# GpSimd's share of the softmax exponentials set to zero, with the planner's constants of that variant

## The chip, the cores and the metric

The kernel runs on one core of a Trainium2 chip. Five engines work side by side on it, each through its own list of instructions in order: TensorE (PE; its weight loads are shown as PEld), VectorE (DVE), ScalarE (ACT), GpSimd (POOL) and SyncE (SP), which here only issues transfers. Semaphores tie the lists together. The metric is the device time of one execution in microseconds (us); the profile is of one execution.

## What is computed

Window attention with cross-shaped stripes on an image of 224 x 224 positions with 96 channels. Half of the channels attend within horizontal stripes of 8 rows, the other half within vertical stripes of 8 columns; then one output projection.

```python
qkv = jnp.einsum('bhwc,cd->bhwd', x, wqkv)          # x: 1 x 224 x 224 x 96
q, k, v = (qkv[..., :C].copy(), qkv[..., C:2 * C].copy(), qkv[..., 2 * C:].copy())
scale = C2 ** (-0.5)                                 # C2 = 48
qh = q[..., :C2].reshape(B * nh, sw * W, C2)         # 28 stripes of 1792 positions
...
ah = _softmax(jnp.einsum('bqc,bkc->bqk', qh, kh) * scale, axis=-1)
oh = jnp.einsum('bqk,bkc->bqc', ah, vh).reshape(B, H, W, C2)
...
av = _softmax(jnp.einsum('bqc,bkc->bqk', qv, kv) * scale, axis=-1)
ov = jnp.einsum('bqk,bkc->bqc', av, vv)              # the same on 28 vertical stripes
...
o = jnp.pad(oh, ((0, 0), (0, 0), (0, 0), (0, C2))) + jnp.pad(ov, ((0, 0), (0, 0), (0, 0), (C2, 0)))
return jnp.einsum('bhwc,cd->bhwd', o, wo)
```

So there are 56 stripes, each with scores of 1792 x 1792, and an exponential of every score.

## The kernel before

**Tiles.** Stripes are worked on in 28 pairs (NP), 14 horizontal, then 14 vertical. Both stripes of a pair share an instruction: one lies in partitions 0 to 63, the other in 64 to 127. The queries of a pair are cut into 4 chunks (512, 512, 512, 256 columns), the keys into 14 tiles of 128. A *score tile* is 128 keys by 512 queries for both stripes (or 2 x 128 keys by 256 queries): 128 partitions by 1024 numbers. A pair has 49 of them (NG), the whole kernel 1372.

**A score tile's way.** TensorE loads key weights (`load_weights`, L190) and multiplies (`loaded_matmul`, L194; for the narrow chunk also L724) into two PSUM banks. Then an exponential is taken in one of three ways:
- ScalarE: one Exp instruction (L892) from banks 0 and 1 or 2 and 3 in turn into one of 8 buffers PTA.
- VectorE: five steps (`d_step`, L903 to L910) that build the bits of a bf16 exponential by a polynomial, from banks 4 and 5 into one of 3 buffers PTD. Steps two to four run in SBUF alone.
- GpSimd: VectorE first copies the tile (L1056) out of banks 4 and 5 to the single buffer `zp_sb` in SBUF, and GpSimd does the polynomial in six steps (`p_step`, L976 to L985), whole or in halves, into one of 3 buffers PTP. At most one such tile is under way.

TensorE then multiplies the result with V (`plan_PV`, L853), summing a chunk's 14 key tiles in bank 6 or 7 (the "value sums"); a column of ones in V gives the softmax's denominator. VectorE empties the bank (L937) into `OT_sb`.

**Fills.** Everything else TensorE does is a `Fill`: the projections of the next pair (K and Q, L462; V, L424) and the output projections of this one (L573, L612). A fill takes the one of banks 6 and 7 that no value sum holds, and its result is taken out by VectorE (L431 for V, L494 and L498 for Q, L506 to L522 for K, L580 and L584 or L618 and L624 for outputs). GpSimd adds the two halves of the output (L647) in the vertical pairs, and SP stores them.

**What sets the order.** The order of each engine is fixed when the kernel is built. A planner walks through an assumed time, and whenever an engine is free in it, asks `pick_act`, `pick_dve`, `pick_pool` or `pick_pe` for its next instruction:
- `pick_pe` takes first ScalarE's next score tile, when its bank is free. Failing that, a tile for GpSimd (while fewer than NPT were given away, L776) or for VectorE (L789), LOOK or LOOKP tiles ahead of ScalarE's; then a value sum, when GRP of them are ready (L816); then a fill. `fits` (L769) lets such work start only if it ends by the time of ScalarE's next tile plus SLACK, or plus DSLACK for VectorE's and GpSimd's tiles.
- Fills have a target before which they don't run and a due time by which they're late (`refill`, L1133): ORD, PACE, DUE1, DUEO, DUES and DUEV set these, and LATE (L815) from when a late one goes ahead of value sums.
- `keep_warm` (L1158) puts spare matmuls into TensorE's gaps when it was idle for more than WARM of the last 3000 ns: a multiplication with zeros added to the open value sum (L1180) or a throw-away product in a free bank (L1199).
- GpSimd's instructions are placed beside VectorE's steps that read PSUM (`safe`, L987), by the assumed time; VectorE's three SBUF steps are held back while the plan has GpSimd busy (L1061).

```python
            if D["cur"] is None and len(P_out) < NZP and D["np"] < NPT and fits(240.0, "r64", DSLACK):
                lo = max(progress(), lastA[0]) + LOOKP
...
            if D["cur"] is None and fits(240.0, "r64", DSLACK):
                G = max(progress(), lastA[0]) + LOOK
...
            late = want_fill and progress() > f.due - LATE and used < NBA - 1
            if ready and fits(235.0) and not late and (len(ready) >= min(GRP, nleft) or used >= NBA - UTH or not want_fill and inburst[0] > 0):
```

When it runs, nothing of the assumed time is left but the order and the semaphores: an instruction waits for what it needs, and those behind it on its engine wait with it.

## Time and profile before

| | |
|---|---|
| three runs | 1096.08, 1096.21, 1099.76 us; median 1096.21 |
| the profiled execution | 1096.08 us, its span 1094.3 us |
| score tiles on ScalarE / VectorE / GpSimd | 1169 / 158 / 45 |
| busy time of GpSimd in its tiles' steps (L976 to L985) | 478.7 us |
| busy time of GpSimd in the output additions (L647) | 105.6 us, 89 instructions |
| VectorE's five steps, mean of one | 1221, 716, 432, 696, 1219 ns |
| TensorE's zeros (L1180) | 34.0 us, 262 matmuls |
| mean granted TensorE clock | 0.993 |

The span runs from the first instruction to the end of the last; the time of the run lies 1.8 us above it. [...] A group's "idle before" is the time its engine stood idle just ahead of the group's instructions, with what ended it.

### The profile page before, as it was taken

The numbers are of one execution on the slowest core, as the hardware profiler recorded it, in microseconds if no ns is written. First come the engines' busy times: TensorE is split into PE (matmuls) and PEld (weight loads), VectorE is DVE, ScalarE is ACT, GpSimd is POOL, SyncE is SP. The second block draws the span as 40 slices with busy tenths as digits, with TensorE's granted clock in tenths as the row PEclk, the third lists the DMA queues.
The fourth block names the chain that finished last, engine by engine and source line by source line (L and its number), as shares of the span: only waits on it lengthen the run. The fifth ranks groups of instructions, "written<-read, shape, count | busy, mean of one in ns | idle before, by whom it ended". The sixth has DMA issues, their size and how long they took to land.

```text
span 1094.3 us, 28704 instructions
## 1 busy us (share of the span) xinstructions
PE 1040.7 (95%) x12104; PEld 372.7 (34%) x12104; DVE 1047.4 (96%) x1712; ACT 1077.2 (98%) x1172; POOL 584.6 (53%) x451
## 2 busy tenths in 40 slices
PE   9999999999999999999999999999999999999997
PEld 2333333332333333233333333333333333333332
DVE  5999999999999999999999999999999999999996
ACT  6999999999999999999999999999999999999997
POOL 0544555453545645364564465656565565656563
PEclk7999999999999999999999999999999999999999
DMA  5301001101110120110111122122222222221111
GB/s 99 69 9 35 19 18 36 36 10 27 36 27 10 35 36 7 30 35 17 20 35 27 35 44 41 39 41 42 41 41 40 39 42 41 39 41 38 24 28 37
DMA packets 169001, 37.37 MB, mean 34 GB/s; under 512 B 168872, under 2 KB 168872, under 8 KB 168872
## 3 DMA queue, kind: packets, MB, share of 16 engines
q1 hardware_dynamic: 167256, 35.35, 17.3%
q8 instruction: 94, 1.54, 0.6%
q10 hardware_dynamic: 1616, 0.18, 0.1%
q14 instruction: 35, 0.29, 0.1%
HBM read 0.15 MB, written 9.63 MB: 9 GB/s over the span
## 4 chain that ended last, share of the span: by engine, by line
ACT 71%; DVE 21%; PE 4%; POOL 1%; issue 1%; DMA 0%; SPq 0%; DVEq 0%; POOLq 0%
ACT PTA L892 71%; DVE tt_sb L903 4%; DVE PTD L910 3%; DVE sq_sb L905 2%; DVE tt_sb L909 2%; PE ps L194 2%; PE ps L853 1%; DVE sq_sb L907 1%; DVE KT_sb L522 1%; DVE zp_sb L1056 1%; DVE tmp L624 1%; DVE OT_sb L937 1%; DVE V_sb L431 1%; POOL PTP L985 1%; DVE QT_sb L498 1%
## 5 line engine op out<-in xcount | busy, mean ns | idle before, releaser
L892 ACT ACTIVATE PTA<-ps 128x1024 bf16<-128x1024 f32 x1169 | 1075.0, 1214 | 5.9 <-PE ps L194 5.1
L194 PE MATMUL ps<-QT_sb,KT_sb 49*64 49x512 bf16 (+3 forms) x5488 | 486.5, 369 | 38.9 <-ACT PTA L892 25.5
L853 PE MATMUL ps<-PTA,V_sb 128*64 128x512 bf16 (+1 forms) x2674 | 422.9, 367 | 0.6 <-DVE Ph_sb L584 0.2
L190 PEld LDWEIGHTS <-KT_sb 49*64 49x64 bf16 (+1 forms) x5488 | 137.4, 103 | 335.0 <-issue 321.9
L903 DVE TENSOR_SCALAR tt_sb<-ps 128x1024 f16<-128x1024 uint16 x158 | 192.9, 1221 | 11.6 <-PE ps L194 7.1
L910 DVE SCALAR_TENSOR_TENSOR PTD<-ps,tt_sb 128x1024 uint16<-128x1024 f32 x158 | 192.5, 1219 | 1.3
L853 PEld LDWEIGHTS ps<-PTA,V_sb 128*64 128x64 bf16 x2674 | 119.8, 108 | 204.1 <-issue 162.8
L647 POOL TENSOR_TENSOR out_sb<-tmp,Ph_sb 128x480 bf16<-128x480 f32 (+2 forms) x89 | 105.6, 1195 | 110.9 <-DVE sq_sb L907 57.9
L978 POOL TENSOR_TENSOR uq_sb<-up_sb 128x1024 f16<-128x1024 f16 (+1 forms) x52 | 101.3, 1952 | 111.6 <-DVE sq_sb L907 57.5
L982 POOL TENSOR_TENSOR up_sb<-uq_sb,up_sb 128x512 f16<-128x512 f16 (+1 forms) x65 | 112.3, 1732 | 84.8 <-DVE sq_sb L907 27.4
L984 POOL TENSOR_TENSOR zp_sb<-zp_sb,up_sb 128x512 f32<-128x512 f32 (+1 forms) x74 | 111.2, 1508 | 54.6 <-DVE sq_sb L907 31.7
L976 POOL TENSOR_SCALAR up_sb<-zp_sb 128x1024 f16<-128x1024 uint16 x45 | 47.1, 1047 | 130.3 <-DVE zp_sb L1056 115.4
L905 DVE TENSOR_TENSOR sq_sb<-tt_sb 128x1024 f16<-128x1024 f16 x158 | 113.1, 716 | 0.1
L909 DVE TENSOR_TENSOR tt_sb<-sq_sb,tt_sb 128x1024 f16<-128x1024 f16 x158 | 109.9, 696 | 2.9
L462 PE MATMUL ps<-xT_sb,w_sb 128*64 128x448 bf16 (+3 forms) x448 | 85.7, 380 | 6.1 <-DVE KT_sb L522 3.0
L937 DVE CAST OT_sb<-ps 128x512 bf16<-128x512 f32 (+5 forms) x118 | 69.3, 591 | 1.4 <-PE ps L853 1.4
L907 DVE TENSOR_SCALAR sq_sb<-sq_sb 128x1024 f16<-128x1024 f16 x158 | 68.2, 432 | 2.2
L1056 DVE COPY zp_sb<-ps 128x1024 f32<-128x1024 f32 x45 | 55.0, 1222 | 8.8 <-POOL PTP L985 4.6
L853 PE MATMUL ps<-PTD,V_sb 128*64 128x512 bf16 (+1 forms) x360 | 62.1, 362 | 0.0
L985 POOL TENSOR_SCALAR PTP<-zp_sb 128x512 uint16<-128x512 f32 (+1 forms) x66 | 57.4, 870 | 5.7 <-POOL zp_sb L984 0.2
L624 DVE TENSOR_TENSOR tmp<-ps,rc 128x480 f32<-128x480 f32 (+2 forms) x92 | 53.2, 578 | 1.1
L522 DVE TENSOR_TENSOR KT_sb<-ps,shift 128x448 bf16<-128x448 f32 (+2 forms) x84 | 51.6, 615 | 2.1 <-PE ps L462 2.1
(55 smaller groups left out, 668.3 us busy)
## 6 DMA issues: line engine op xcount, KB each, us to landing
out_dram<-out_sb SPq DMA_DIRECT2D x389, 24.0 KB, 1.9
xT_sb<-in_x_dram SPq DMA_TRANSPOSE x332, 2.6
w_sb<-in_wqkv_dram ACTq DMA_DIRECT2D x2, 54.0 KB, 3.1
out_dram<-out_sb ACTq DMA_DIRECT2D x3, 24.0 KB, 1.9
wo_sb<-in_wo_dram SPq DMA_DIRECT2D x4, 9.0 KB
wo_sb<-one_sb SPq DMA_DIRECT2D x4, 0.0 KB
```

Source lines behind the costliest of these rows:

```text
L190: return e.add_instruction(mybir.InstLdweights(tile_size=(64, 64), tile_position=pos, name=nc.get_next_instruction_name(), engine=mybir.En ...
L194: return e.add_instruction(mybir.InstMatmult(start_tensor_calc=True, stop_tensor_calc=True, tile_size=(64, 64), tile_position=pos, ldweigh ...
L647: return e.tensor_tensor(out_sb[b][:, wdw, k0:k0 + n, :], tmpi[:, 0:n, :], Ph_sb[:, k0:k0 + n, j, :], ALU.add)
L853: ins = e.matmul(bk[64 * wdw:64 * wdw + 64, 0:qs], lhsT=V_sb[b][:, wdw, kt, :], rhs=pt[:, wdw * 512 + i * qs:wdw * 512 + (i + 1) * qs], st ...
L892: e = add("act", [ev, bufA_ev[sl]], lambda e, base=base, sl=sl: e.activation(PTA[sl][:], ps[:, base * 512:(base + 2) * 512], ACTF.Exp, sca ...
L903: return lambda e: e.tensor_scalar(tt_sb[:], dps.bitcast(U16)[:, 0:2048:2], CS / 65536.0, CS * CA3, ALU.mult, ALU.add)
L905: return lambda e: e.tensor_tensor(sq_sb[:], tt_sb[:], tt_sb[:], ALU.mult)
L909: return lambda e: e.tensor_tensor(tt_sb[:], sq_sb[:], tt_sb[:], ALU.mult)
L910: return lambda e: e.scalar_tensor_tensor(PTD[sl][:].bitcast(U16), dps, CC, tt_sb[:], ALU.add, ALU.add)
L978: return e.tensor_tensor(q, u, u, ALU.mult)
L982: return e.tensor_tensor(u, q, u, ALU.mult)
L984: return e.tensor_tensor(z, z, u, ALU.add)
```

## The change

Only constants at the head of the kernel differ; no function does. NPT = 0 means that no score tile goes to GpSimd. The rest are the planner's: SLACK, WARM and the like keep their value and become floats; DSLACK goes from 120 to 300, GRP from 2 to 3, LOOK from 8 to 10, PACE from 1 to 1.5, LATE from 10 to 5; ORD = 0 puts the first two Q fills ahead of the V fills and reckons due times back from the end of the pair, where ORD = 1 has all K and Q fills due from the pair's beginning. LOOKP is without effect once NPT is 0, and DUE1 and DUEV once ORD is 0; DUEO then counts.

```diff
-    SLACK = 120
-    PACE = 1
+    SLACK = 120.0
+    PACE = 1.5
     FDUE = 20.0
-    DSLACK = 120.0
-    GRP = 2
+    DSLACK = 300.0
+    GRP = 3
     NBA = 8
-    LOOK = 8
-    NPT = 400
+    LOOK = 10
+    NPT = 0
...
-    DUE1 = 0
+    DUE1 = 20.0
     DUEV = 10
-    LATE = 10
+    LATE = 5.0
...
-    ORD = 1
-    LOOKP = 32
-    WARM = 600
+    ORD = 0
+    LOOKP = 16
+    WARM = 600.0
```

The kernel that results from it, as built, has 1195 score tiles on ScalarE, 177 on VectorE and none on GpSimd.

## The prediction

> **What bounds the kernel now.** I read the page first: busy shares, then the chain of waits, then the groups by line, then a window without start and end.

> ```profile
> span 1094.3 us, 28704 instructions
> PE 1040.7 (95%) x12104; PEld 372.7 (34%) x12104; DVE 1047.4 (96%) x1712; ACT 1077.2 (98%) x1172; POOL 584.6 (53%) x451
> ...
> ACT 71%; DVE 21%; PE 4%; POOL 1%; issue 1%; DMA 0%; SPq 0%; DVEq 0%; POOLq 0%
> ...
> L892 ACT ACTIVATE PTA<-ps 128x1024 bf16<-128x1024 f32 x1169 | 1075.0, 1214 | 5.9 <-PE ps L194 5.1
> ...
> L903 DVE TENSOR_SCALAR tt_sb<-ps 128x1024 f16<-128x1024 uint16 x158 | 192.9, 1221 | 11.6 <-PE ps L194 7.1
> ...
> L1056 DVE COPY zp_sb<-ps 128x1024 f32<-128x1024 f32 x45 | 55.0, 1222 | 8.8 <-POOL PTP L985 4.6
> ```

> ```profile
> 30.00:1060.00 1030.00, 986.28 (x11621) 354.66 (x11619) 1004.21 (x1616) 1029.35 (x1122) 565.57 (x422) 1.00 0.17 32
> ```

> The second fence is the window from 30 to 1060 us: PE, PEld, DVE, ACT, POOL busy, then the granted clock, 1.00. ScalarE is never idle there (1029.35 of 1030), VectorE hardly (97.5%). ScalarE's busy time hides small losses, because its instructions overlap: one lasts 1214 ns on average, yet the next starts earlier. The timeline shows by how much.

> ```profile
> 8.40 1.94 ACT L892 ACTIVATE PTA<-ps 128x1024 bf16<-128x1024 f32 x2 [1.03 <-PE ps L194]
> ...
> 1070.79 1.83 POOL L985 TENSOR_SCALAR PTP<-zp_sb 128x512 uint16<-128x512 f32 x2
> ...
> 1071.58 0.57 DVE L907 TENSOR_SCALAR sq_sb<-sq_sb 128x1024 f16<-128x1024 f16 x1
> ...
> 1072.18 0.97 DVE L909 TENSOR_TENSOR tt_sb<-sq_sb,tt_sb 128x1024 f16<-128x1024 f16 x1
> ...
> 1072.68 0.41 PE L853 MATMUL ps<-PTP,V_sb 128*64 128x512 bf16 x2 [0.60 <-POOL PTP L985]
> ...
> 1073.46 14.77 ACT L892 ACTIVATE PTA<-ps 128x1024 bf16<-128x1024 f32 x16 [0.18 <-PE ps L194]
> ...
> 1078.24 0.68 DVE L909 TENSOR_TENSOR tt_sb<-sq_sb,tt_sb 128x1024 f16<-128x1024 f16 x1
> ```

> Sixteen score tiles in 14.77 us, less 1.21 for the last, are 13.56 / 15 = 0.904 us from start to start; no interval of the 1168 in the trace is shorter, and over half equal it. That is ScalarE's floor. The first tile starts at 8.40, the last at 1073.46 + 14.77 - 1.19 = 1087.04, so 1168 intervals took 1078.6 us where the floor is 1055.9: 22.8 us are lost. The 14th tile starts at 25.50 (the long ScalarE stretch of the chain begins there), so 17.10 - 13 x 0.904 = 5.4 us of it are lost at the start and 17.4 later. The fence also shows two ways of losing: TensorE waits 0.60 us for a tile from GpSimd, and the score tile queued behind it comes late; and a GpSimd instruction over SBUF-only VectorE work stretches L909 from 0.68 to 0.97.

> **What is removed.** NPT = 0 takes away all of GpSimd's 45 score tiles: on VectorE 45 copies (L1056), on GpSimd 353 half- or full-tile steps (L976 to L985, 479 us busy), on TensorE 51 pairs of value-sum matmuls that read PTP. The built program shows who inherits them. ScalarE's tiles go from 1169 to 1195, VectorE's own from 158 to 177: 26 + 19 = 45. TensorE's matmuls are the same but for zeros (131 to 180 pairs at L1180) and padding (8 to 15 at L1199). All projection and output work, SP's queue and its order are identical.

> **ScalarE's sum.** 26 more tiles at the floor: 26 x 0.904 = +23.5 us. Nothing can cover it, since the engine has no idle time in the window above. [...]

> **VectorE's sum.** A copy holds it 1.14 us (start to next start, back to back): 45 x 1.14 = -51.3. A tile of its own holds it 1.140 + 0.609 + 0.343 + 0.609 + 1.132 = 3.83 (medians of L903, L905, L907, L909, L910, the same way): 19 x 3.83 = +72.8. GpSimd's overlaps go: L905 lasts 685 ns alone and 853 under L985 (21 times), 866 under L980 (6); L907 422 alone, 504 under L985 (12); L513 328 alone, about 960 under GpSimd (5). With the few L909 like the one above that is some 11 us; the 89 additions L647 stay and keep 2, so -9. Its waits for GpSimd's single zp_sb buffer and around the copies (7.7 in all) go, and the rest of its mid-span waits (18.2) grow with 177/158, +2.2. Sum: -51.3 + 72.8 - 9 - 5.5 = +7. So ScalarE asks for 23.5 more and VectorE for 7; ScalarE becomes the clearer bound, and VectorE gets some 16 us of slack.

> [...]

> **The lost 17.4.** A score tile's matmuls (L194) start 50 ns after ScalarE has left their bank, and ScalarE starts 425 ns after they do; with 1231 ns for its own instruction that is 1706 against 2 x 0.904 = 1808: a cover of 0.10 us. TensorE runs in order, so whatever is late in front of a score tile by more eats ScalarE's time. In the trace 7.8 us of the loss stands behind a TensorE wait that a VectorE instruction ended (KT_sb L522 alone 3.5). The stretches holding a GpSimd tile's value sums lose 1.97 us in 45, where others lose 14 ns each, so 1.3 goes with them for certain. The relief lies between -1.3 and -17.4; I take 1.3 and six tenths of the 7.8, together -6, as VectorE gets slack but keeps its order and its waits.

> **The other constants.** DSLACK (120 to 300), GRP, LOOK, PACE, LATE and ORD move work between the score tiles; I read what stands between two of ScalarE's in TensorE's order. It is still at most two items ("value sum, value sum" 406 times before, 428 after), so no stretch holds more than before. A VectorE score tile stands directly in front of ScalarE's 85 times, against 63. Such stretches lose 5 ns each now. A tile's matmuls hold TensorE 0.21 us (two value-sum pairs take 0.62, one takes 0.41), so with the cover gone each costs 0.11: from 22 x 0.005 = 0.1 to 85 x 0.11 = +9.4. I take +1, by the nearest row, that of the same stretches. Filling work in last place goes from 137 to 146 stretches, 46 ns each against 16 in first place: +0.3, left out. More zeros fill gaps; stretches ending in zeros lose 0 to 9 ns now, so nothing. The bound on all of this below is nought, since a gain is counted in the relief. TensorE's order is the same for the first 14 score tiles, so the 5.4 of the start stays; the end, six microseconds after the last score tile, keeps its work.

> **Sum.** 1094.3 + 23.5 - 6 + 1 = 1112.8 us of span. Around the span lie 1096.08 - 1094.3 = 1.8, and that run is within 0.2 of the median 1096.21. Forecast: **1114.6**.

> **The rivals.**
> - *VectorE's relief goes all to ScalarE.* For it: the chain passes through VectorE for 21%, and VectorE is 97.5% busy. Against it: of 13.3 us in the intervals that lose over 20 ns each, 4.9 stand behind no wait of TensorE for VectorE or GpSimd. The loss falls by 12 to 17.4: 1094.3 + 23.5 - 12 (or 17.4) + 1.8 = 1107.6 to 1102.2.
> - *VectorE's tiles push ScalarE's.* DSLACK 300 lets L789's pick stand closer in front of a score tile; behind it are queued the score tile and the value sums, and for those ScalarE's buffers wait. For it: the 85 places and a cover of only 0.10. Against it: 5 ns each today. With no relief beyond 1.3: 1094.3 + 23.5 - 1.3 + 9.4 + 1.8 = 1127.7; from 1122.
> - *Not slower.* ScalarE's waits all came from the mixed work of three engines, and with GpSimd out it runs at its floor throughout: 1094.3 + 23.5 - 22.8 + 1.8 = 1096.8. Against 0.5% (5.5 us, about what a measurement here can tell from no change) it counts as no change while the whole loss stays under 4.9 us. The start alone loses 5.4 and its order is unchanged.
> - *It does not do what its few words say.* Bank choice (L304), the first four score tiles (L1097) and the zeros (L1172) are in both kernels; only constants differ. That moves no number, as the counts above are of the built programs.

> **How the numbers follow.** Forecast 0.56 (own range 1109 to 1121, from relief of 12 with +1 to relief of 1.3 with 22 x 0.11 = 2.4 pushed: 1119.6 - 11 and + 1.1), relief 0.20, pushed tiles 0.21, not slower 0.03. The range goes from 1104 (leaving the lower third of the relief case and the last one, about 0.1) to 1126 (leaving under half of the pushed case, about 0.1). Slower by over 0.5% means above 1101.7: 0.96; within 0.5%: 0.03; faster: 0.01, since it would need ScalarE under its floor.

> **What would show it.** After: L892 x1195 with the floor interval still 0.904; no L1056 and no L976 to L985; L903 x177; VectorE's share in the middle at 96 to 97%, L905's mean near 690 instead of 716; ScalarE's loss after the 14th tile at 10 to 14 us. It is wrong if the floor moves, if ScalarE loses under 6 or over 24 us there, or if ScalarE waits for anything but score tiles.

## The result, and the profile after

The changed kernel takes 1114.17 us (median of 4 runs, 1113.07 to 1117.7) against 1096.26 for the kernel before (4 runs): ratio 1.0161, with a 95% interval from 1.0130 to 1.0193. The profiled execution took 1115.08 us, its span 1112.8. The forecast was 1114.6 with a span of 1112.8. The span came out as forecast; outside it lie 2.2 to 2.4 us in the four runs of the changed kernel, where the forecast kept the 1.8 of before. What fills that time the traces don't show.

The page of the changed kernel, in the order in which the page of before was read (span, busy times, chain by engine and by line, groups):

```profile
span 1112.8 us, 28395 instructions
PE 1051.7 (95%) x12209; PEld 378.6 (34%) x12209; DVE 1064.1 (96%) x1762; ACT 1098.4 (99%) x1198; POOL 105.4 (9%) x98
...
ACT 97%; PE 1%; DMA 0%; SPq 0%; DVE 0%; issue 0%
...
L892 ACT ACTIVATE PTA<-ps 128x1024 bf16<-128x1024 f32 x1195 | 1096.3, 1299 | 2.7 <-PE ps L194 2.6
...
L903 DVE TENSOR_SCALAR tt_sb<-ps 128x1024 f16<-128x1024 uint16 x177 | 216.2, 1221 | 18.2 <-PE ps L194 12.4
...
L905 DVE TENSOR_TENSOR sq_sb<-tt_sb 128x1024 f16<-128x1024 f16 x177 | 121.3, 686 | 0.5
```

GpSimd has only its output additions left. The chain of waits, of which VectorE had 21% before, is now ScalarE's from end to end (97%). L905 is down from 716 ns to 686; before, it lasted 685 where no GpSimd instruction lay over it.

**The account that should have been made.** The prediction counted ScalarE from start to start. For its row of tiles that is not the right measure, and the prediction's own example shows why: the row of 16 score tiles in 14.77 us. Read one by one in the trace, their starts are 0.904 us apart, but their durations grow from 1018 ns for the second to 1192 for the last, by 12.5 at every tile. A tile that is ready starts a little earlier relative to its predecessor's end each time, and finishes no sooner. From end to end the row gives (14.77 - 1.02) / 15 = 0.917. The timeline of ScalarE near the end of the changed kernel shows the same over 150 tiles:

```profile
968.73 137.93 ACT L892 ACTIVATE PTA<-ps 128x1024 bf16<-128x1024 f32 x150
```

The first of these lasts 1.35 us, so (137.93 - 1.35) / 149 = 0.9166. In both traces the intervals between ends that stay under 925 ns average 0.9166 us (1131 of 1168 before and 1187 of 1194 after are such); eight before and two after are below 914 ns. The starts are 0.904 apart only until a tile lasts some 1357 ns. Then it waits for its bank (50 ns) and its matmuls (425), and 1357 + 50 + 425 = 1832 for two tiles is again 0.916. So the floor is 0.9166, and the same figure stands in the kernel: the planner reckons 917.0 ns for a score tile on ScalarE (L893). The account by ends is (us):

| | before | after |
|---|---|---|
| end of the first score tile | 9.4 | 9.7 |
| further tiles x 0.9166 | 1168: 1070.6 | 1194: 1094.4 |
| lost in the first 13 intervals | 5.2 | 2.5 |
| lost after 30 us | 3.0 | 0.0 |
| after the last score tile | 6.0 | 6.2 |
| span | 1094.3 | 1112.8 |

The change is +0.3 + 23.8 - 2.7 - 3.0 + 0.1 = +18.5. Two terms need a cause: the 3.0 us that went (25 intervals over 940 ns before, none after), and the 2.7 at the start, where TensorE's order is the same in both.

**The start.** A granted clock of 1.00 is called whole here, one of 0.50 half. These are the windows from 0 to 11, 11 to 25 and 25 to 35 us of the kernel before, then 11 to 20 us of the changed one (PE, PEld, DVE, ACT, POOL busy, then the granted clock):

```profile
0.00:11.00 11.00, 8.38 (x58) 3.30 (x58) 3.99 (x18) 4.47 (x6) 1.61 (x9) 1.00 0.68 118
11.00:25.00 14.00, 14.00 (x86) 3.21 (x84) 9.28 (x18) 10.36 (x11) 0.00 (x0) 0.51 0.45 85
25.00:35.00 10.00, 10.00 (x104) 3.11 (x102) 9.00 (x14) 9.94 (x12) 5.37 (x5) 1.00 0.27 51
```

```profile
11.00:20.00 9.00, 8.98 (x66) 2.16 (x66) 5.73 (x12) 7.32 (x8) 0.00 (x0) 0.62 0.44 79
```

The granted clock is at half for 13.65 us in the one (11.09 to 24.74) and for 6.83 in the other (12.04 to 18.87). ScalarE's loss there, 5.2 and 2.5, stands in the same proportion, 0.38 and 0.36 us for each us at half clock. The traces of the experiments below agree. Three more have a half clock at the start: 3.8 us are lost for 10.24 (e3_load_after), 5.1 for 13.65 (e4_load_before) and 2.4 for 6.83 (e8_load30_before). Four have a whole clock there with nothing done to the start (e1_npt0, e2_gp_back, e5_nzp2, e7_load30_after), and lose 0 to 0.2.

### The profile page after: what moved, and what is told of

Its sections match the earlier page's. It is cut to its first block, busy times and chain, and to the rows that moved or that the text cites. A ratio compares the mean times of both kernels' runs of the same rounds, so it can differ in the third digit from the quotient of the medians.

```text
span 1112.8 us, 28395 instructions
## 1 busy us (share of the span) xinstructions
PE 1051.7 (95%) x12209; PEld 378.6 (34%) x12209; DVE 1064.1 (96%) x1762; ACT 1098.4 (99%) x1198; POOL 105.4 (9%) x98
## 4 chain that ended last, share of the span: by engine, by line
ACT 97%; PE 1%; DMA 0%; SPq 0%; DVE 0%; issue 0%
ACT PTA L892 97%; PE ps L194 0%; DMA xT_sb<-in_x_dram 0%; PE ps L853 0%; SPq L201 0%; PE ps L462 0%; PE ps L424 0%; DVE tmp L624 0%; DVE out_sb L647 0%; PE ps L612 0%; PE ps L1199 0%; DVE OT_sb L937 0%; DVE rc L618 0%; PE ps L724 0%
## 5 line engine op out<-in xcount | busy, mean ns | idle before, releaser
L892 ACT ACTIVATE PTA<-ps 128x1024 bf16<-128x1024 f32 x1195 | 1096.3, 1299 | 2.7 <-PE ps L194 2.6
L194 PE MATMUL ps<-QT_sb,KT_sb 49*64 49x512 bf16 (+3 forms) x5488 | 482.7, 364 | 53.4 <-ACT PTA L892 39.2
L853 PE MATMUL ps<-PTA,V_sb 128*64 128x512 bf16 (+1 forms) x2732 | 418.2, 365 | 0.7 <-DVE Ph_sb L584 0.4
L903 DVE TENSOR_SCALAR tt_sb<-ps 128x1024 f16<-128x1024 uint16 x177 | 216.2, 1221 | 18.2 <-PE ps L194 12.4
L910 DVE SCALAR_TENSOR_TENSOR PTD<-ps,tt_sb 128x1024 uint16<-128x1024 f32 x177 | 215.8, 1219 | 2.0
L647 POOL TENSOR_TENSOR out_sb<-tmp,Ph_sb 128x480 bf16<-128x480 f32 (+2 forms) x89 | 103.8, 1181 | 1001.7 <-DVE OT_sb L937 654.9
L853 PEld LDWEIGHTS ps<-PTA,V_sb 128*64 128x64 bf16 x2732 | 118.5, 108 | 194.7 <-issue 142.0
L909 DVE TENSOR_TENSOR tt_sb<-sq_sb,tt_sb 128x1024 f16<-128x1024 f16 x177 | 121.8, 688 | 3.7
L905 DVE TENSOR_TENSOR sq_sb<-tt_sb 128x1024 f16<-128x1024 f16 x177 | 121.3, 686 | 0.5
L907 DVE TENSOR_SCALAR sq_sb<-sq_sb 128x1024 f16<-128x1024 f16 x177 | 74.6, 421 | 2.6
L853 PE MATMUL ps<-PTD,V_sb 128*64 128x512 bf16 (+1 forms) x404 | 70.4, 366 | 0.0
L522 DVE TENSOR_TENSOR KT_sb<-ps,shift 128x448 bf16<-128x448 f32 (+2 forms) x84 | 51.7, 616 | 2.0 <-PE ps L462 1.9
L724 PE MATMUL ps<-QT_sb,KT_sb 49*64 49x256 bf16 (+1 forms) x784 | 53.5, 268 | 0.0
L584 DVE TENSOR_TENSOR Ph_sb<-ps,rc 128x480 bf16<-128x480 f32 x84 | 51.9, 618 | 0.6
L431 DVE CAST V_sb<-ps 128x480 bf16<-128x480 f32 (+1 forms) x84 | 51.7, 617 | 0.3
L1180 PE MATMUL ps<-warm,ident 128*64 128x256 bf16 x360 | 47.5, 283 | 0.0
L462 PEld LDWEIGHTS ps<-xT_sb,w_sb 128*64 128x64 bf16 (+1 forms) x448 | 24.8, 106 | 53.9 <-issue 28.9
L498 DVE SCALAR_TENSOR_TENSOR QT_sb<-ps,biasq 128x448 bf16<-128x448 f32 (+2 forms) x59 | 36.3, 616 | 1.8 <-PE ps L462 1.8
```

Of the source, the lines that this page charges most:

```text
L194: return e.add_instruction(mybir.InstMatmult(start_tensor_calc=True, stop_tensor_calc=True, tile_size=(64, 64), tile_position=pos, ldweigh ...
L462: ins = e.matmul(o, lhsT=wS[0:kr, wblk(P, kind), :], rhs=x_cols(wdw), start=True, stop=True)
L647: return e.tensor_tensor(out_sb[b][:, wdw, k0:k0 + n, :], tmpi[:, 0:n, :], Ph_sb[:, k0:k0 + n, j, :], ALU.add)
L853: ins = e.matmul(bk[64 * wdw:64 * wdw + 64, 0:qs], lhsT=V_sb[b][:, wdw, kt, :], rhs=pt[:, wdw * 512 + i * qs:wdw * 512 + (i + 1) * qs], st ...
L892: e = add("act", [ev, bufA_ev[sl]], lambda e, base=base, sl=sl: e.activation(PTA[sl][:], ps[:, base * 512:(base + 2) * 512], ACTF.Exp, sca ...
L903: return lambda e: e.tensor_scalar(tt_sb[:], dps.bitcast(U16)[:, 0:2048:2], CS / 65536.0, CS * CA3, ALU.mult, ALU.add)
```

## The experiments

In all of them "loss" is ScalarE's time by ends above 0.9166 for each interval. Line numbers shift by one or two where lines were added.

**GpSimd's tiles or the other constants?**

```diff
 # e1_npt0, on the kernel before
-    NPT = 400
+    NPT = 0
 # e2_gp_back, on the changed kernel
-    NPT = 0
+    NPT = 400
-    LOOKP = 16
+    LOOKP = 32
```

> The kernel before with one constant changed, NPT = 0; it has 1195 score tiles on ScalarE, as the changed kernel. Theory A (ScalarE's score tiles end 0.917 us apart whatever stands between them, so the number of its tiles sets the time): 26 x 0.917 = +23.8 us over the kernel before, less up to 3.0 us of its later waits if those came with GpSimd's tiles: 1117 to 1120 us, within 3 us of the changed kernel's 1114.2. Theory B (the other constants, DSLACK and the order of the fills above all, are what made the later waits vanish): ScalarE still loses about 3 us after the first 30 us, at the same kind of places in every fourth pair, and the run is 3 us or more above the changed kernel.

Measured: 1116.35 us (1113.03 to 1118.89), ratio to the kernel before 1.0193 (1.0162 to 1.0225). ScalarE's loss after 30 us is 0.04 us, with every other constant as before. So with the old constants the waits of 3.0 us come and go with GpSimd's tiles, and the other constants aren't needed to remove them.

> The changed kernel with NPT = 400 and LOOKP = 32, so with GpSimd's tiles back and all other constants as changed; it has 1179 score tiles on ScalarE, 165 on VectorE, 28 on GpSimd. Theory A: 16 tiles fewer than the changed kernel, 1114.2 - 16 x 0.917 = 1099.5 us, plus later waits of 0 to 3. Theory B (the other constants cost or gain something by themselves): more than 3 us off that. If waits of ScalarE after 30 us come back, they belong to GpSimd's tiles; if they stay at nought, to the kernel before's own constants.

Measured: 1108.3 us, ratio 1.0141 (1.0100 to 1.0181): 8.8 above theory A's 1099.5, so the count alone did not hold. The timeline of ScalarE shows where it is, and then a window (PE, PEld, DVE, ACT, POOL busy, granted clock):

```profile
153.46 1.02 ACT L892 ACTIVATE PTA<-ps 128x1024 bf16<-128x1024 f32 x1 [0.38 <-PE ps L194]
154.97 1.02 ACT L892 ACTIVATE PTA<-ps 128x1024 bf16<-128x1024 f32 x1 [0.49 <-PE ps L194]
156.53 1.02 ACT L892 ACTIVATE PTA<-ps 128x1024 bf16<-128x1024 f32 x1 [0.54 <-PE ps L194]
```

```profile
152.00:170.00 18.00, 17.56 (x146) 5.64 (x150) 12.76 (x19) 12.19 (x13) 1.84 (x2) 0.53 0.01 2
```

From 152.7 to 169.8 us the clock is at half, score tiles come 1.5 us apart, and ScalarE loses 7.4 us there; elsewhere after the start it loses nothing. The span also ends 2.6 us later behind the last score tile (8.7 us for 6.2). GpSimd's tiles by themselves, 28 of them here, left no waits at a whole clock. So the 3.0 us of the kernel before take both: GpSimd's tiles, and either its own constants or the larger number, 45. These two runs don't tell which of the latter. In the 3 us before 152.7 TensorE waited 0.22 us for KT_sb, 0.31 for ScalarE to leave a bank and 0.77 for OT_sb; what made these late, and whether the clock fell because of them, is open too.

**How much room does VectorE have?** An idle fill of a scratch tile is put into VectorE's list, with no wait and no semaphore, so the order of everything else is untouched.

```diff
                     k = d["k"]
+                    if k == 4 and D["n"] % 3 == 0:
+                        ops["dve"].append(([], lambda e: e.memset(junk[:], 0.0), False))
                     ev = add("dve", ws, d_step(k, sl), D_OCC[k], D_OCC[k] + 107.0)
```

> The changed kernel with 59 idle fills of a scratch tile (128 x 388) put into VectorE's list, one ahead of L910 of every third of its own tiles: 59 x 0.33 = about 19 us more work on VectorE and nothing else. Theory of the forecast (VectorE is 97% busy and near to being the bound, with some 16 us of room): up to 5 us longer. Theory A (only ScalarE sets the pace and VectorE's lateness is caught by the buffers ahead): below 2 us, ScalarE's loss after 30 us still under 2. Rival (VectorE is the bound as well): the whole 19.

> The same idle fills in the kernel before: 53 x 0.33 = about 17 us more work on VectorE. Theory of the forecast (VectorE and ScalarE bound it together, VectorE having hardly any room): 8 to 17 us longer. Theory A (ScalarE sets the pace in the kernel before too, to within 3.0 us of waits after the start): under 4 us longer. The difference between this and the same load in the changed kernel is the room that the change gave VectorE.

The load was smaller than planned: a fill lasted 0.22 us, and no run shows the 0.33 that was expected. So there were 13.0 us of durations in the changed kernel and 11.7 in the kernel before. A fill overlaps its neighbours, so VectorE's busy time rose less, by 4.9 us (1064.1 to 1069.0) and 4.8 (1047.4 to 1052.2). Measured: 1117.7 us (1112.37 to 1122.34) and 1094.42 (ratio to the kernel before 1.0001, 0.9982 to 1.0020). ScalarE's loss after 30 us stays at 0.01 in the first; its profile, of the run of 1116.7, lost 3.8 at the start, at half clock, and the one run with a mean clock of 0.998 took 1112.37. In the second the loss after 30 us goes from 3.0 to 4.2. VectorE, 97.9 and 97.8% busy between 30 and 1060 us, does not set the time by itself in either. The 8 to 17 us for the kernel before were expected of a larger load than this one turned out to be. A larger load (1064 columns for 388) was needed to find the room:

> The changed kernel with larger idle fills on VectorE (128 x 1064), again one ahead of L910 of every third of its tiles: 59 x 0.45 to 0.5 = about 28 us of work, as much as VectorE's idle time between 30 us and the end (27). The smaller load of 8 us left ScalarE's loss there at nought. Theory A: VectorE's room is its idle time, so 0 to 8 us longer. Rival (VectorE co-bound): 15 to 28 us.

> The same larger fills in the kernel before: 53 x 0.45 to 0.5 = about 25 us of work, VectorE's idle time there being 26 us. The smaller load took ScalarE's loss after 30 us from 3.0 to 4.2 us. If GpSimd's tiles made VectorE tight (forecast), this costs clearly more than in the changed kernel: 8 to 20 us. If VectorE had as much room as there: under 8 us.

Measured: 1122.08 us (ratio to the kernel before 1.0276, 1.0242 to 1.0311) and 1106.49 (1.0121, 1.0095 to 1.0146). The page's busy times, the group of the fill, and ScalarE's wait (line, waited for: us, times, longest), of the changed kernel with this load, and then the same of the kernel before with it:

```profile
PE 1050.1 (94%) x12209; PEld 376.9 (34%) x12209; DVE 1081.5 (97%) x1821; ACT 1103.0 (99%) x1198; POOL 105.5 (9%) x98
...
L1077 DVE MEMSET junk<- 128x532 uint32 x59 | 29.6, 502 | 3.5
```

```profile
ACT PTA L893 <- PE ps L195: 2.3, 6, 1.0
```

```profile
PE 1042.9 (94%) x12104; PEld 371.1 (34%) x12104; DVE 1064.0 (96%) x1765; ACT 1083.2 (98%) x1172; POOL 584.0 (53%) x451
...
L1077 DVE MEMSET junk<- 128x532 uint32 x53 | 26.6, 502 | 3.2
```

```profile
ACT PTA L893 <- PE ps L195: 6.8, 21, 1.0
```

ScalarE's loss after 30 us goes from 0.0 to 8.0 us, and from 3.0 to 15.1. VectorE's busy time rose by 17.4 us (1064.1 to 1081.5) and 16.6 (1047.4 to 1064.0). So 9.4 us are hidden in the changed kernel and 4.5 in the kernel before; by the fills' durations, 29.6 and 26.6, it would be 21.6 and 14.5. Either way the change gave VectorE room, an estimated 5 to 7 us from these two loads of unequal size. The kernel before, with 12.1 us more loss, lies where it was expected if GpSimd's tiles made VectorE tight (8 to 20).

**Is the start the clock's doing?** Four throw-away matmuls are put where TensorE stands idle after the first two score tiles; they carry no semaphore, so nothing else moves.

```diff
+        for _ in range(4):
+            ops["pe"].append(([e_warm], lambda e: e.matmul(bank(4)[:, :], lhsT=warm[:, 0:128], rhs=warm[:, :], start=True, stop=True), False))
         for f in [pf0["K"][1], pf0["V"][0]]:
```

> The kernel before with four more throw-away matmuls on zeros in the gap that TensorE has after the first two score tiles; nothing else differs. Theory C (what ScalarE loses in its first 13 intervals, 5.2 us in the kernel before's profile and 2.5 in the changed one's, is the TensorE clock at half for 13.7 and 6.8 us there, which the thin work of the first 11 us brings about or not from launch to launch): the granted clock stays whole at the start in most runs, ScalarE's loss there falls under 1 us, and the median falls by 2 to 5 us with less spread. Rival (the loss is that of the order there, waiting for x and the first projections): unchanged to 1 us.

Measured: ten runs between 1091.5 and 1092.77 us, where 13 of the kernel before beside them lay between 1091.39 and 1095.82, in two heaps: seven up to 1091.83, six from 1093.56. Ratio 0.9989 (0.9977 to 1.0001). The profile has a whole clock and ScalarE loses 0.6 us at the start:

```profile
11.00:25.00 14.00, 13.19 (x138) 4.02 (x138) 12.79 (x24) 13.96 (x16) 2.08 (x2) 1.00 0.46 87
```

Theory C's cause holds: the spread went, and of the runs beside it the seven low ones had a mean granted clock of 0.998 or 0.999, the six high ones 0.993 to 0.997. The median did not fall by 2 to 5 us, as seven of the 13 runs beside it were low ones. With this start the two sides of the change can be compared with a whole clock on both:

> The kernel before with NPT = 0 and the four matmuls at the start: the price of GpSimd's tiles alone, with the clock whole at the start. 26 x 0.917 = +23.8 less the 2.9 us of waits that go: +20.9 over the kernel before with the same start (1091.95): 1112.9, spread under 2 us.

> The changed kernel with the four matmuls at the start. If the other constants do nothing to the time, the same as the run with NPT = 0 alone and this start, 1112.9, to 1 us; ScalarE's loss at the start under 1 us and after 30 us under 0.5.

Measured: 1113.24 us (1112.88 to 1113.81) for the kernel before with NPT = 0, 1113.1 (1112.77 to 1114.1) for the changed kernel, ratios to the kernel before 1.0180 (1.0160 to 1.0201) and 1.0180 (1.0159 to 1.0201). Against 1091.95 that is +21.3 and +21.2 where +20.9 was expected. The 1091.95 comes from another round, on another chip; beside these two runs the kernel before had three with a clock of 0.999, at 1090.95, 1091.46 and 1091.65, and against the middle one it is +21.8 and +21.6. ScalarE loses 1.2 and 0.5 us at the start and 0.04 and 0.01 after 30 us; why 1.2, at a whole clock, is open. With no tile on GpSimd, the other constants together do nothing that these runs can tell.

**More tiles for GpSimd?** If ScalarE's count set the time, giving GpSimd more tiles, or sooner ones that leave ScalarE fewer, should beat both kernels.

```diff
 # e5_nzp2
-    NZP = 1
+    NZP = 2
 # e9_lookp24_start (and 18 in e10_lookp18_start), with the four matmuls at the start
-    LOOKP = 32
+    LOOKP = 24
```

> The kernel before with two zp_sb buffers instead of one (NZP = 2), so that two of GpSimd's tiles can be under way: 1150 score tiles on ScalarE, 158 on VectorE, 64 on GpSimd. Theory A (ScalarE's tiles end 0.917 us apart, their number sets the time): 19 tiles fewer, -17.4 us, plus later waits of ScalarE of 3 to 6 us instead of 3: 1077 to 1081 us. Rival (VectorE is the bound with ScalarE; 19 more copies of 1.14 us and more of GpSimd's overlaps cost it 22 us and more): no gain, or slower than the kernel before.

> The kernel before with the four matmuls at the start and LOOKP = 24 for 32: 1164 score tiles on ScalarE, 164 on VectorE, 44 on GpSimd. By the count of ScalarE's tiles 5 x 0.917 = 4.6 us below the kernel before with the same start (1091.95): 1087.4, if ScalarE's waits after 30 us stay near 3 us. If GpSimd's tiles, taken 8 score tiles later than before, come too late for their value sums, ScalarE waits 5 us or more and the gain is lost.

> The same with LOOKP = 18: 1162 score tiles on ScalarE, 161 on VectorE, 49 on GpSimd. By the count 7 x 0.917 = 6.4 us below 1091.95: 1085.5. GpSimd's tiles have still less time here (18 score tiles, some 14 us, for about 12 us of steps that wait for VectorE's), so waits of ScalarE of 5 to 30 us at their value sums are as likely, which would put it above the kernel before.

Measured: 1161.08, 1172.79 and 1151.53 us, ratios 1.0635 (1.0603 to 1.0668), 1.0734 (1.0697 to 1.0770) and 1.0522 (1.0487 to 1.0558). ScalarE's loss after 30 us is 88, 80 and 62 us. Here are ScalarE's waits in the run with two buffers, and then, from the view of the tile PTP, who waited for it (us, times):

```profile
ACT PTA L892 <- PE ps L853: 58.4, 21, 8.1
ACT PTA L892 <- PE ps L194: 20.1, 28, 1.4
```

```profile
  PEld ps L853: 17.1, 28
  DVE zp_sb L1056: 9.3, 10
  PE ps L853: 8.6, 19
```

TensorE's weight loads stand 17.1 us, and within that its matmuls 8.6 us, before value sums of a GpSimd tile that isn't finished. The value sums behind them wait too, and ScalarE, which needs a buffer that value sums free, stops for up to 8.1 us at a time. The clock falls as well: it is at half for 68, 133 and 58 us of these three runs. Of ScalarE's loss some 34 of 88, 60 of 80 and 30 of 62 us lie in those stretches, an interval across an edge being divided by time. With LOOKP = 24 the loads stand only 2.9 us before a PTP tile, so most of that loss is at half clock, and nothing here shows that late tiles brought the clock down. No version beat the kernel before.

## Why the prediction was right, and where it was not

**The count.** 26 score tiles more on ScalarE with nothing to cover them make +23.8 us, of which the 3.0 of waits that went are taken off; this held in the three other kernels without GpSimd's tiles and without a load (e1_npt0, e11_npt0_start, e12_after_start). The price was mis-sized a little: 0.904 us a tile taken from starts, 0.9166 by ends, so 23.8 for 23.5.

**"The lost 17.4".** This step failed. It was the difference between the two ways of counting, summed over 1155 intervals: by ends the kernel before loses 3.0 us after the start, not 17.4. By the prediction's own count the changed kernel still "loses" 14.7 there, just above the 10 to 14 that it gave as a sign, while by ends it loses nothing.

**The relief of 6.** The mechanism (waits that come with GpSimd's tiles go) was right and is shown by the kernel with NPT = 0 alone, but it can't be larger than 3.0, and it is 3.0. One such wait can be followed in the trace of before:

```profile
977.87 2.53 POOL L647 TENSOR_TENSOR out_sb<-tmp,Ph_sb 128x480 bf16<-128x480 f32 x2 [3.32 <-DVE KT_sb L506]
...
979.56 0.97 DVE L513 TENSOR_SCALAR KT_sb<-KT_sb,shift 128x448 bf16<-128x448 bf16 x1
...
984.38 0.38 PE L462 MATMUL ps<-xT_sb,w_sb 128*64 128x448 bf16 x2 [0.24 <-DVE KT_sb L522]
```

L513 lasts 0.97 us under GpSimd's addition, where it takes 0.33 alone; the K fills after it run late, TensorE waits for one, and the score tile at 986.16 ends 0.23 late. In the changed kernel no L513 lies under GpSimd any more and all 28 average 330 ns. The order of this chain is read from one place. The kernel before has five L513 that last 0.95 to 0.97 us, and 6.6 to 6.7 us after the start of each ends one of the 25 late tiles; these five lose 1.0 us of the 3.0 together. The cause of the other 20 is open.

**"The 5.4 of the start stays".** It did not, in the profiled pair: 2.5 for 5.2. This 2.7 happened to fill the place of the relief that wasn't there, so that the total came out within 0.5 us is partly luck. With a whole clock on both sides the profiled spans are 1089.7 (the kernel before with the four matmuls) and 1110.5 (the changed kernel with them): +20.8, where 18.5 was forecast. The three mis-sized terms account for that: 0.3 more for the count, 3.0 less relief, 1.0 less for pushed tiles. The run times differ by 21 to 22 us, which is still within the stated range.

**VectorE's sum of +7.** Its busy time rose by 16.7 us (1047.4 to 1064.1), where the terms for work came to 72.8 - 51.3 - 9 = 12.5. Its waits between 30 us and the last 25 did not fall by 5.5 but stayed (25.9 to 27.0 us): those for GpSimd went, and the idle time before L903, most of it for its matmuls, took their place (9.6 to 16.1). VectorE's waits after the change, longest first:

```profile
DVE tt_sb L903 <- PE ps L194: 12.4, 38, 1.4
DVE rc L618 <- PE ps L612: 6.2, 6, 1.8
...
DVE tt_sb L903 <- PE ps L724: 1.7, 3, 0.6
```

Its share of the window from 30 to 1060 us is 97.5% as before, not the 96 to 97 forecast. It did get room, an estimated 5 to 7 us by the loads, not 16.

**The pushed tiles, +1.** Nothing: by ends the changed kernel loses 0.0 us after the start with its 85 tiles in front of ScalarE's. In these rows a tile's end stays 0.9166 after the one before it whether the tile lasts 1018 ns or 1357, so its start can come up to 0.34 us later at no cost; the start-to-start count took that reserve for loss.

**The rivals.** "Relief goes all to ScalarE" was right in kind, since the later loss did vanish, and wrong in size for the same reason as the 17.4. "Not slower" had its mechanism right: after the start ScalarE does run at its floor throughout. But what could be won was 8.2 us (5.2 at the start and 3.0 later), not 22.8, and so the 23.8 for the tiles could not be covered. That only constants changed, and that the three new-sounding parts stand in both kernels, was right.

**GpSimd's overlaps.** VectorE got back what the rows said: the means of L905, L907, L909 and L513 fell by 30, 11, 8 and 111 ns, which over their counts in the kernel before is some 11 us.

## What to carry to other kernels

Take an engine's floor from end to end, in long rows, and check it by the total: in these rows a start-to-start spacing below it (0.904 us for 0.9166) only showed instructions that began earlier while their durations grew. An engine at 97% need not be the bound (VectorE with the small load in the changed kernel: 97.9% busy, and ScalarE lost 0.01 us); adding idle work to it and watching the bounding engine's loss gives an idea of its room, but count the work by the rise of busy time. The number of tiles taken off the bounding engine decides only while the order around them holds: 45 tiles on GpSimd saved 21 us, and 64 were 69 us slower than the 45, with late tiles and a half clock together.

## What the runs showed of the hardware

How full a stretch between two multiples was is worked out from the matmuls' starts, those side by side counted once, with 0.21 us for 512 columns (L194 in the kernel before: starts at 7.96 and 8.17 us). The first fall came after a stretch that was filled to 0.44 (before), 0.47 (after), 0.37 (e2_gp_back) and 0.47 to 0.48 (the two small loads and e8_load30_before). Stretches from 0.46 on were passed at a whole clock in e1_npt0, e2_gp_back and e8_load30_before. In the three slow kernels with more or sooner GpSimd tiles, falls followed stretches of 0.31 to 0.46, and some from 0.41 on were passed. So the filling alone does not tell a fall from none in these runs: 0.46 and some from 0.41 on were passed, 0.44 and 0.47 were not.

The same order had mean clocks from 0.993 to 0.999 in the 13 runs of the kernel before beside e6_start. What decides it is not shown, as each kernel has one trace; that it is where the multiples lie against the start is the author's estimate, from the 4.26 and 5.21 us. A half clock at the start, at some 0.37 us of ScalarE's time for each us, is what made the kernel before's runs differ by 4 us (1091.39 to 1095.82); with the four matmuls and a whole clock they lay within 1.3.
